# Value rows with a row sum beside each half, and the normalisation of the attention output once a chunk

## The chip, the cores and the metric

The kernel runs on one core of a Trainium2 chip. TensorE (PE) multiplies matrices into PSUM, VectorE (DVE) and ScalarE (ACT) compute on SBUF and PSUM, GpSimd (POOL) makes masks and issues some transfers, and SyncE (SP) issues most transfers. Each engine works through its own queue in order. The metric is device time in microseconds; less is better.

## What is computed

Two independent layers share the launch, and their results stand side by side in the output. The first is causal attention with a sliding window of 256 positions, 32 heads of 32 columns, 2048 positions:

```
qkv = (x @ wqkv).reshape(B, S, 3, H, Dh)
scores = einsum("bhqd,bhkd->bhqk", q, k) * Dh**-0.5
mask = (i - j >= 0) & (i - j < 256)
p = softmax(where(mask, scores, -1e9));  o = einsum("bhqk,bhkd->bhqd", p, v)
a = o.reshape(B, S, D) @ wo
```

The second is a Fourier mixing layer by matrices: a product along the hidden axis (real and imaginary part), then one along the sequence, of which the real part is kept:

```
a = x @ dft_hid_re.T;  b = x @ dft_hid_im.T
y = dft_seq_re @ a - dft_seq_im @ b
```

All is wanted to float32 precision. The kernel splits a float32 operand into two f16 parts, high and low, and forms three of the four products of parts (PASSES, L45).

## The kernel before

The work falls into stages on TensorE. First come the query, key and value projections (function `product`, L341, called from the loop at L710). Their results are split into high and low parts and written to scratch in DRAM: queries and keys to `qs`, values to `vs`. Then come the units of the Fourier layer (loop at L916): for each of two passes p (real, imaginary) and two column halves c, eight hidden-axis units `x` (`product` again, tile `p`) and eight sequence units `c` (function `seven`, L813, tiles `p_a`, `p_b`, `p_c`, a scheme of seven instead of eight block products). Last come the units of the output projection (`po_a`, `po_b`, `po_c`).

Attention is woven into these stages. It is a generator (`attention`, L175), and `tick` (L325) advances it by one step after a given number of matmuls of the other work. It goes through blocks of 128 queries for a pair of heads, in the order group of four heads (8), chunk of 512 positions (4), head pair (2), block in the chunk (4): 256 blocks, 32 chunks of eight blocks.

For a block, `s_step` (L197) forms the scores in PSUM, VectorE masks and takes the row maximum (L222, L224), ScalarE takes the exponential in place (L234) and copies the high half to f16 (L237), VectorE forms the low half (L238), and SyncE issues a transposing transfer of both halves into the tile `t` (L240). Three blocks later `z_step` (L243) lets POOL mask the edges of the window (L252, L254). Six blocks later (LAG, L39) `v_step` (L258) works on two blocks at a time: TensorE multiplies the transposed weights by the value rows `vt` (L282).

A value row of a head has 65 columns: low half (32), high half (32), and a one. High weights multiply all 65 columns; low weights multiply the last 33, high half and one. So after the products a PSUM row of 65 holds two partial results of 32 and the sum of the weights. VectorE then takes the reciprocal of the sums (L288), adds the two partial results, PSUM to PSUM (L290), and multiplies by the reciprocal into the chunk's tile `o` in SBUF (L293). The value bank has one buffer (`ps_v`, tag "pv"), shared with the small transposes `pt_...` by which scales are found (L147, L148).

After a chunk, `o_step` (L298) splits `o` into high and low f16 parts (ScalarE L302, VectorE L303), SyncE issues a transposing transfer (L305) and a store to the scratch `ots` (L306), from which the output projection reads much later.

The value rows are made at L720 to L733: POOL writes the ones (L726), ScalarE the high half (L729), VectorE the low half (L730), and SyncE stores them (L732). `do_load` brings them back a chunk at a time (L193).

The order of instructions in each engine's queue is laid out by a planner, which simulates the whole program with costs of its own (`schedule_with_timeline_sim`, L1021); `issue_after` pins a few pairs. In the sequence units of all but the first group (first pass, first column half), POOL also issues the transfers that add onto the output (L909).

Of the kernel before, what the change touches and what calls it, by code (L numbers as in the profile page):

```python
# [9 lines left out]
F32 = mybir.dt.float32  # L10
F32R = mybir.dt.float32r
F16 = mybir.dt.float16
# [3 lines left out]
AF = mybir.ActivationFunctionType  # L16
ALU = mybir.AluOpType
AX = mybir.AxisListType

P = 128  # L20
# [3 lines left out]
DH = 32  # L24
HG = 4
# [3 lines left out]
CH = 512  # L29
NCH = S // CH  # L30
QB = CH // P
VW = 2 * DH + 1
SCALE = DH ** -0.5
PSHIFT = 15.0 * math.log(2.0)
NEG = -1.0e30
# [1 line left out]
WARM = 32  # L37

LAG = 6  # L39
VW = 2 * DH + 1  # L40

# [7 lines left out]
def fused_kernel(ctx: ExitStack, tc: tile.TileContext, xa, wqk, wv, wo, xb, wd, cs, out):  # L51
    nc = tc.nc
    PSUM = bass.MemoryType.PSUM

    qs = tc.dram_tile((2, NG, NCH, 2, P, CH), F16, name="qs")
    vs = tc.dram_tile((NT, P, H * VW), F16, name="vs")
    ots = tc.dram_tile((NCH, P, NG, 2, CH), F16, name="ots")
# [35 lines left out]
    def bank(name):  # L93
        nbank[0] += 1
        return ps_m.tile([P, CH], F32, tag=f"m{nbank[0] % 3}", name=name)
# [9 lines left out]
    def vec(f, *args, **kwargs):  # L105
        with tc.issue_after(latest[0].ins) if strict[0] and latest else nullcontext():
            latest[:] = [f(*args, **kwargs)]
        return latest[0]
# [15 lines left out]
    behind = []  # L124
# [50 lines left out]
    def attention():  # L175
        att = cell["att"]
# [3 lines left out]
        st, cur, q2s, k2s, vts = {}, {}, {}, {}, {}  # L180

        def do_load(g, sc):
            if (g, sc) in q2s:
                return
            for d, kind, parts, bufs in ((k2s, 1, (0, 0, 1), 3), (q2s, 0, (0, 1, 0), 2)):
                u = att.tile([96, HG, CH], F16, tag=f"qk{kind}", bufs=bufs, name=f"qk{kind}_{g}_{sc}")
                for j, part in enumerate(parts):
# [3 lines left out]

            vt = att.tile([P, QB, HG * VW], F16, tag="vt", bufs=3, name=f"vt_{g}_{sc}")
            nc.sync.dma_start(vt, vs[sc * QB:sc * QB + QB, :, g * HG * VW:(g + 1) * HG * VW]  # L193
                              .rearrange("t p c -> p t c"))
# [63 lines left out]
        def v_step(b):  # L258

            g, sc, hp, i = blocks[b]  # L260
            pvb = ps_v.tile([P, CH], F32, tag="pv", name=f"pv_{b}")
            pvt = pvb[:, :4 * VW].rearrange("p (r h w) -> p r h w", r=2, h=2)
            if (g, sc) not in cur:
                cur[g, sc] = att.tile([P, QB, P], F32, tag="o", bufs=3, name=f"o_{g}_{sc}")
            for r in (1, 0):
                qb = sc * QB + i + r
                nb = min(qb + 1, 3)
                nt = min(nb, 2)
                d = st[b + r]

                def weights(part, j, kb):
                    if nb == 3 and kb == 0:
                        return d["z"][:, part * 2 + j]
                    return d["t"][:, (part * 2 + j) * nt + kb - (nb - nt)]

                seq = [(0, kb) for kb in range(nb)] + [(1, kb) for kb in range(nb)]
                for j in range(2):
                    at = (2 * hp + j) * VW
                    for m, (part, kb) in enumerate(seq):
                        lo = DH * part  # L280
                        k = qb + 1 - nb + kb
                        nc.tensor.matmul(pvt[:, r, j, lo:], weights(part, j, kb),  # L282
                                         vts[g, k // QB][:, k % QB, at + lo:at + VW],
                                         start=(m == 0), stop=(m == len(seq) - 1),
                                         skip_group_check=True)
            o = cur[g, sc]
            rs = att.tile([P, 2, 2], F32, tag="rs", name=f"rs_{b}")
            nc.vector.reciprocal(rs, pvt[:, :, :, 2 * DH])  # L288
            os_ = pvb[:, 4 * VW:4 * VW + 4 * DH].rearrange("p (r h d) -> p r h d", r=2, h=2)
            nc.vector.tensor_reduce(os_.rearrange("p r h d -> p (r h) d"),  # L290
                                    pvt[:, :, :, :2 * DH].rearrange("p r h (k d) -> p (r h) d k", k=2),
                                    axis=AX.X, op=ALU.add)
            nc.vector.tensor_tensor(  # L293
                o[:, i:i + 2, hp * 64:hp * 64 + 64].rearrange("p r (h d) -> p r h d", d=DH), os_,
                rs.unsqueeze(3).to_broadcast([P, 2, 2, DH]), op=ALU.mult)
            del st[b], st[b + 1]

        def o_step(g, sc):  # L298

            o = cur.pop((g, sc)).rearrange("p i c -> p (i c)")  # L300
            ohl = att.tile([P, 2, CH], F16, tag="o", bufs=3, name=f"ohl_{g}_{sc}")
            nc.scalar.activation(ohl[:, 0], o, AF.Copy)  # L302
            nc.vector.tensor_tensor(ohl[:, 1], o, ohl[:, 0], op=ALU.subtract)  # L303
            ot = att.tile([P, 2 * QB, P], F16, tag="o", bufs=3, name=f"ot_{g}_{sc}")
            nc.sync.dma_start_transpose(ot, ohl.rearrange("p h c -> p (h c)"))  # L305
            nc.sync.dma_start(ots[sc, :, g].rearrange("c h t -> c (h t)"), ot.rearrange("p a q -> p (a q)"))  # L306

        for b in range(nblk + LAG):
            for j in range(2):
# [6 lines left out]
                if j == 0 and b % 2 == 0 and b >= LAG:  # L316
                    v_step(b - LAG)
                    g, sc, hp, i = blocks[b - LAG + 1]
# [22 lines left out]
    def product(ps, lhs, rhs, n=ND, gate=None):  # L341

        m = 0
        for d in range(n):
            for hl, hr in PASSES:
                with tc.issue_after(gate.ins) if gate and 2 * d == n else nullcontext():
                    nc.tensor.matmul(ps, lhs(hl, d), rhs(hr, d), start=(m == 0), stop=(m == 3 * n - 1))  # L347
                m += 1
                if m % 8 == 0:
                    tick(8)  # L350
# [146 lines left out]
    behind_act = []  # L497
# [51 lines left out]
    for n in range(len(scans)):  # L549
        at(21 + n, scan_load, n)  # L550
        at(22 + n, scan_top, n)
        key, _, _, i, k = scans[n]
# [156 lines left out]
    with tc.tile_pool(name="pa", bufs=2) as pa:  # L709
        for n, (kd, g, c) in enumerate(order):  # L710
            if n == 4:
                first_cm.__exit__(None, None, None)
                att_cm = tc.tile_pool(name="att", bufs=2, side="right")
                cell["att"] = att_cm.__enter__()
            if n == START:
                agen[0] = attention()
                upcoming[0] = next(agen[0])
            for f, args in tasks.pop(n, ()):
                f(*args)
            ps = bank(f"p{kd}{g}_{c}")  # L720
            if kd == "v":
                t = c
                product(ps, lambda h, d: xin[:, t // 4, h, d, t % 4 * P:t % 4 * P + P],
                        lambda h, d: reg2[:, g, h, d])
                y = pa.tile([P, H // 2, VW], F16, tag="yv", name=f"yv{g}_{t}")
                nc.gpsimd.memset(y[:, :, 2 * DH:], 1.0)  # L726
                f = vf[:, g, t // 4:t // 4 + 1]
                pv = ps.rearrange("p (h d) -> p h d", d=DH)
                behind_act[:] = [nc.scalar.activation(y[:, :, DH:2 * DH], pv, AF.Copy, scale=f)]  # L729
                behind[:] = [nc.vector.scalar_tensor_tensor(y[:, :, :DH], pv, f, y[:, :, DH:2 * DH],  # L730
                                                            op0=ALU.mult, op1=ALU.subtract)]
                nc.sync.dma_start(vs[t, :, g * (H // 2) * VW:(g + 1) * (H // 2) * VW],  # L732
                                  y.rearrange("p h w -> p (h w)"))  # L733
            else:
                u = wun[kd, g]
                product(ps, lambda h, d: u[:, h, d], lambda h, d: xin[:, c, h, d], gate=gates.get(n))
                y = pa.tile([P, 2, CH], F16, tag="yq", name=f"y{kd}{g}_{c}")
                f = DOWN if kd == "q" else kf[:, c:c + 1]
                behind_act[:] = [nc.scalar.activation(y[:, 0], ps, AF.Copy, scale=f)]
                behind[:] = [vec(nc.vector.scalar_tensor_tensor, y[:, 1], ps, f, y[:, 0],  # L740
                                 op0=ALU.mult, op1=ALU.subtract)]
                nc.sync.dma_start(qs["qk".index(kd), g, c].rearrange("j p t -> p j t"), y)
            if kd == "v" and g == 0 and c % 4 == 3:
                ready.add((0, c // 4))
            if kd == "v" and g == 1 and c == NT - 1:
                pass
            if kd == "k" and g > 0:
                ready.add((g, c))
# [31 lines left out]
    os_, oq = {}, {}  # L780
# [69 lines left out]
    with tc.tile_pool(name="pb", bufs=1) as pb:  # L850
# [65 lines left out]
        for n, (kind, p, c, i) in enumerate(units):  # L916
            if kind == "x":
                x = uns.pop(n)
                tb = ytile()
                k = i % 4  # L920
# [10 lines left out]
                else:  # L931
                    a = pair.pop()
# [23 lines left out]
            f = fu.pop(n)  # L956
# [68 lines left out]
```

## Time and profile before

| | us |
|---|---|
| median of three runs | 1834.63 |
| lowest and highest | 1828.07, 1836.04 |
| span of the profiled execution | 1822.3 |
| PE busy | 1756.3 (96%) |
| DVE busy | 1325.8 (73%) |
| ACT busy | 1093.0 (60%) |
| POOL busy | 406.9 (22%) |

The profile comes from one execution. Its span runs from the first to the last instruction; the execution's own whole time is not on the page, and the median of the runs lies 12.3 us above the span. An engine that is busy is not always useful, and one that idles is not always in the way: what counts is where TensorE, the busiest engine, waits, and what ends the wait. Groups of instructions are named by line, engine and operation, with "out<-in" by the program's tile names. The mean granted clock of TensorE is 0.989 of full speed.

### The profile page before, as it was taken

To read this page: it belongs to the slowest core of one execution; us is meant where nothing else is said; L and a number is where in the kernel's file an instruction comes from. 1 tells how busy PE (TensorE), PEld (TensorE's weight loads), DVE (VectorE), ACT (ScalarE), POOL (GpSimd) and SP (SyncE) were. 2 spreads that over 40 slices of the span, in tenths; PEclk is the share of its full clock that TensorE was granted. 3 is DMA by queue.
4 is the path that set the end of the run, shared out by engine and by line. 5 is a ranking of instruction groups with operands and counts; after the bars stand their busy time and mean duration, and the time that the engine had idled before them with its cause. 6 is when DMAs were issued, how large, how long until landed. Compare 5 with 4: busy or idle time off the path is not lost.

```text
span 1822.3 us, 30052 instructions
## 1 busy us (share of the span) xinstructions
PE 1756.3 (96%) x10876; PEld 857.3 (47%) x10876; DVE 1325.8 (73%) x2362; ACT 1093.0 (60%) x1867; POOL 406.9 (22%) x666
## 2 busy tenths in 40 slices
PE   7999999999999999999989899998989999999998
PEld 3444545555545544555444444544544554444443
DVE  7665887778766788886788686888876788577442
ACT  3333554556556777776777676777776678463322
POOL 0000222222212222322123233323333223200000
PEclk9999999999999999999999999999999999999999
DMA  5357898978767656899548989756998746855331
GB/s 231 115 176 209 211 249 216 237 176 215 183 144 166 128 123 156 183 197 214 111 100 173 197 182 199 162 127 128 188 176 191 151 93 128 226 109 98 110 93 70
DMA packets 440598, 297.96 MB, mean 164 GB/s; under 512 B 339072, under 2 KB 396416, under 8 KB 440448
## 3 DMA queue, kind: packets, MB, share of 16 engines
q1 hardware_dynamic: 433536, 270.87, 62.1%
q0 software_dynamic: 6912, 25.17, 8.4%
q8 instruction: 85, 1.39, 0.3%
q14 instruction: 65, 0.53, 0.1%
HBM read 146.93 MB, written 75.63 MB: 122 GB/s over the span
## 4 chain that ended last, share of the span: by engine, by line
PE 73%; DVE 9%; issue 7%; DMA 6%; ACT 4%; POOL 2%; SPq 0%; POOLq 0%; DVEq 0%; ACTq 0%
PE p L347 13%; PE p_a L825 10%; PE pv L347 9%; PE pk L347 9%; PE pq L347 8%; PE p_b L825 5%; PE po_a L825 5%; DMA t<-hl 3%; PE s L214 3%; PE pv L282 3%; PE p_c L825 3%; PE po_b L825 2%; PE po_c L825 1%; DVE raw_u L626 1%; DMA out_dram<-reg 1%
## 5 line engine op out<-in xcount | busy, mean ns | idle before, releaser
L347 PE MATMUL p<-reg,un 128*128 128x512 f16 x1536 | 345.1, 379 | 0.0
L234 ACT ACTIVATE s<-s,bias,escs 128x256 f32<-128x256 f32 (+1 forms) x512 | 267.4, 528 | 10.6
L227 ACT ACTIVATE bias<-mx,pshift,escs 128x2 f32<-128x2 f32 x256 | 97.5, 383 | 242.7 <-DVE mx L224 210.8
L231 POOL TENSOR_SCALAR mark<-bias 128x1 f32<-128x1 f32 x128 | 42.8, 334 | 846.0 <-ACT bias L227 831.5
L347 PEld LDWEIGHTS <-un 128*128 128x128 f16 x1536 | 146.5, 98 | 164.9
L238 DVE TENSOR_TENSOR hl<-s,hl 128x512 f16<-128x512 f32 (+1 forms) x256 | 169.7, 666 | 74.5 <-ACT hl L237 72.5
L825 PE MATMUL p_a<-reg,un_c 128*128 128x512 f16 x768 | 186.0, 384 | 6.4 <-ACT p_c L832 4.9
L347 PE MATMUL pq<-reg,wu_q 128*128 128x512 f16 x768 | 177.8, 386 | 6.9 <-ACT reg L113 4.3
L254 POOL TENSOR_SCALAR_AFFINE_SELECT t<-t 128x512 f16<-128x512 f16 x224 | 181.2, 881 | 0.1
L347 PE MATMUL pk<-reg,wu_k 128*128 128x512 f16 x768 | 175.1, 379 | 0.9 <-ACT wu_k L113 0.5
L347 PE MATMUL pv<-reg,reg 128*128 128x512 f16 x768 | 174.0, 379 | 0.0
L224 DVE TENSOR_REDUCE mx<-s 128x2 f32<-128x512 f32 (+1 forms) x256 | 169.5, 666 | 2.4
L252 POOL TENSOR_SCALAR_AFFINE_SELECT z<-t 128x512 f16<-128x512 f16 x224 | 155.4, 712 | 48.9 <-DMA t<-hl 48.3
L237 ACT ACTIVATE hl<-s 128x512 f16<-128x512 f32 (+1 forms) x256 | 148.3, 583 | 9.8 <-DMA t<-hl 5.0
L222 DVE COPY_PREDICATED s<-upper,s 128x256 f32<-128x256 uint32 x224 | 94.0, 422 | 60.1 <-PE s L214 55.5
L214 PE MATMUL s<-qk,qk 96*128 96x128 f16 (+2 forms) x704 | 128.7, 276 | 3.4 <-DVE hl L238 3.4
L282 PE MATMUL pv<-vt,t 128*128 128x65 f16 x1984 | 114.3, 186 | 11.6 <-POOL t L254 11.2
L347 PEld LDWEIGHTS <-wu_q 128*128 128x128 f16 x768 | 75.3, 99 | 96.0 <-issue 13.2
L825 PEld LDWEIGHTS <-un_a 128*128 128x128 f16 x768 | 74.8, 99 | 93.1 <-issue 8.5
L825 PEld LDWEIGHTS <-un_c 128*128 128x128 f16 x768 | 74.4, 99 | 92.6 <-issue 10.2
L825 PEld LDWEIGHTS <-un_b 128*128 128x128 f16 x768 | 73.4, 98 | 89.2 <-issue 5.3
L282 PEld LDWEIGHTS <-t 128*128 128x128 f16 x1984 | 97.8, 97 | 35.1 <-POOL t L254 14.9
(175 smaller groups left out, 2873.1 us busy)
## 6 DMA issues: line engine op xcount, KB each, us to landing
raw_u<-in_cs_dram SPq DMA_DIRECT2D x64, 512.0 KB, 4.8
qk<-qs SPq DMA_DIRECT2D x192, 128.0 KB, 3.2
out_dram<-y POOLq DMA_DIRECT2D x36, 512.0 KB, 7.5
raw_u<-in_xb_dram SPq DMA_DIRECT2D x32, 512.0 KB, 5.2
vs<-yv SPq DMA_DIRECT2D x32, 260.0 KB, 2.8
vt<-vs SPq DMA_DIRECT2D x32, 260.0 KB, 4.3
raw_x<-in_xa_dram SPq DMA_DIRECT2D x16, 512.0 KB, 10.2
qs<-yq SPq DMA_DIRECT2D x32, 256.0 KB, 2.2
```

What stands on the lines that cost most here:

```text
L214: nc.tensor.matmul(s[:, j, at:at + (k1 - k0) * P], q2s[g, sc][:, h, i * P:i * P + P], k2s[g, k0 // QB][:, h, k0 % QB * P:k0 % QB * P + (k1 ...
L222: nc.vector.copy_predicated(s[:, :, 2 * P:3 * P], upper2, s[:, :, :P] if nb == 3 else never2)
L224: nc.vector.tensor_reduce(mx, sv, axis=AX.X, op=ALU.max, negate=True)
L227: nc.scalar.activation(bias, mx, AF.Identity, bias=pshift, scale=es)
L234: nc.scalar.activation(sv[:, h], sv[:, h], AF.Exp, bias=bias[:, h:h + 1], scale=es)
L237: nc.scalar.activation(hi, sv, AF.Copy)
L238: behind[:] = [nc.vector.tensor_tensor(lo, sv, hi, op=ALU.subtract)]
L252: nc.gpsimd.affine_select(out=z, in_=pk, compare_op=ALU.is_gt, fill=0.0, base=0, pattern=[[0, 4], [-1, P]], channel_multiplier=1)
L254: nc.gpsimd.affine_select(out=pk, in_=pk, compare_op=ALU.is_ge, fill=0.0, base=0, pattern=[[0, 4], [1, P]], channel_multiplier=-1)
L282: nc.tensor.matmul(pvt[:, r, j, lo:], weights(part, j, kb), vts[g, k // QB][:, k % QB, at + lo:at + VW], start=(m == 0), stop=(m == len(se ...
L347: nc.tensor.matmul(ps, lhs(hl, d), rhs(hr, d), start=(m == 0), stop=(m == 3 * n - 1))
L825: nc.tensor.matmul(ps, lhs[pos](hl, k), rhs(pos)[:, hr, k], start=(m == 0 and pos < 2), stop=(m == 11), skip_group_check=True)
```

## The change

A value row of a head becomes 66 columns: high half (32), one, low half (32), zero. High weights multiply all 66 columns; low weights the first 33. The two halves of a PSUM row then have the same form, 32 partial results and a partial sum of weights, the second of which is zero. One VectorE addition over the two halves gives results and sum of weights together, 33 columns a head, and writes them to the chunk's tile `o` in SBUF, which grows from 128 to 4 x 33 columns a block. The reciprocal and the multiplication move from `v_step`, where they ran for every two blocks, to `o_step`, where they run once a chunk, in place, over all four blocks and four heads. POOL fills the zero column with a second memset.

```diff
-VW = 2 * DH + 1
+VW = 2 * DH + 2
...
-                cur[g, sc] = att.tile([P, QB, P], F32, tag="o", bufs=3, name=f"o_{g}_{sc}")
+                cur[g, sc] = att.tile([P, QB, HG, DH + 1], F32, tag="o", bufs=3, name=f"o_{g}_{sc}")
...
-                        lo = DH * part
+                        w = VW if part == 0 else DH + 1
                         k = qb + 1 - nb + kb
-                        nc.tensor.matmul(pvt[:, r, j, lo:], weights(part, j, kb),
-                                         vts[g, k // QB][:, k % QB, at + lo:at + VW],
+                        nc.tensor.matmul(pvt[:, r, j, :w], weights(part, j, kb),
+                                         vts[g, k // QB][:, k % QB, at:at + w],
...
-            rs = att.tile([P, 2, 2], F32, tag="rs", name=f"rs_{b}")
-            nc.vector.reciprocal(rs, pvt[:, :, :, 2 * DH])
-            os_ = pvb[:, 4 * VW:4 * VW + 4 * DH].rearrange("p (r h d) -> p r h d", r=2, h=2)
-            nc.vector.tensor_reduce(os_.rearrange("p r h d -> p (r h) d"),
-                                    pvt[:, :, :, :2 * DH].rearrange("p r h (k d) -> p (r h) d k", k=2),
+            nc.vector.tensor_reduce(o[:, i:i + 2, 2 * hp:2 * hp + 2], pvt.rearrange("p r h (k w) -> p r h w k", k=2),
                                     axis=AX.X, op=ALU.add)
-            nc.vector.tensor_tensor(
-                o[:, i:i + 2, hp * 64:hp * 64 + 64].rearrange("p r (h d) -> p r h d", d=DH), os_,
-                rs.unsqueeze(3).to_broadcast([P, 2, 2, DH]), op=ALU.mult)
...
         def o_step(g, sc):
-            o = cur.pop((g, sc)).rearrange("p i c -> p (i c)")
-            ohl = att.tile([P, 2, CH], F16, tag="o", bufs=3, name=f"ohl_{g}_{sc}")
+            o = cur.pop((g, sc)).rearrange("p i h w -> p (i h) w")
+            rs = att.tile([P, HG * QB], F32, tag="rs", name=f"rs_{g}_{sc}")
+            nc.vector.reciprocal(rs, o[:, :, DH])
+            o = o[:, :, :DH]
+            nc.vector.tensor_tensor(o, o, rs.unsqueeze(2).to_broadcast([P, HG * QB, DH]), op=ALU.mult)
+            ohl = att.tile([P, 2, HG * QB, DH], F16, tag="o", bufs=3, name=f"ohl_{g}_{sc}")
             nc.scalar.activation(ohl[:, 0], o, AF.Copy)
             nc.vector.tensor_tensor(ohl[:, 1], o, ohl[:, 0], op=ALU.subtract)
...
-                nc.gpsimd.memset(y[:, :, 2 * DH:], 1.0)
+                nc.gpsimd.memset(y[:, :, DH:DH + 1], 1.0)
+                nc.gpsimd.memset(y[:, :, 2 * DH + 1:], 0.0)
...
-                behind_act[:] = [nc.scalar.activation(y[:, :, DH:2 * DH], pv, AF.Copy, scale=f)]
-                behind[:] = [nc.vector.scalar_tensor_tensor(y[:, :, :DH], pv, f, y[:, :, DH:2 * DH],
+                behind_act[:] = [nc.scalar.activation(y[:, :, :DH], pv, AF.Copy, scale=f)]
+                behind[:] = [nc.vector.scalar_tensor_tensor(y[:, :, DH + 1:2 * DH + 1], pv, f, y[:, :, :DH],
```

More of the change, by code (lines that the diff above doesn't have):

```diff
@@ L39 @@
 LAG = 6
-VW = 2 * DH + 1
+VW = 2 * DH + 2
 PASSES = ((0, 0), (0, 1), (1, 0))
@@ L304, in o_step @@
             ot = att.tile([P, 2 * QB, P], F16, tag="o", bufs=3, name=f"ot_{g}_{sc}")
-            nc.sync.dma_start_transpose(ot, ohl.rearrange("p h c -> p (h c)"))
+            nc.sync.dma_start_transpose(ot, ohl.rearrange("p a i d -> p (a i d)"))
             nc.sync.dma_start(ots[sc, :, g].rearrange("c h t -> c (h t)"), ot.rearrange("p a q -> p (a q)"))
```

## The prediction

> **What bounds the kernel now.** I read the page's first and fourth parts, then stage by stage the busy time of each engine, then who waits for whom on TensorE and on SyncE's queue, and last the groups whose instructions the change touches. First the page:
>
> ```profile
> span 1822.3 us, 30052 instructions
> PE 1756.3 (96%) x10876; PEld 857.3 (47%) x10876; DVE 1325.8 (73%) x2362; ACT 1093.0 (60%) x1867; POOL 406.9 (22%) x666
> ...
> PE 73%; DVE 9%; issue 7%; DMA 6%; ACT 4%; POOL 2%; SPq 0%; POOLq 0%; DVEq 0%; ACTq 0%
> ```
>
> TensorE is busy 96% of the span and carries 73% of the chain that ended last; the changed lines are all on VectorE, which carries 9%. So the change can only pay through the 66 us in which TensorE stands still (1822.3 - 1756.3). Where those lie (columns: stretch, length, then busy time of PE, PEld, DVE, ACT, POOL with instruction counts, granted clock, DMA share and rate):
>
> ```profile
> 682.00:832.00 150.00, 149.28 (x1003) 75.33 (x1003) 124.45 (x241) 117.71 (x209) 42.18 (x64) 1.00 0.82 188
> 909.00:1136.00 227.00, 206.89 (x1374) 101.84 (x1373) 179.25 (x326) 160.66 (x281) 74.61 (x101) 0.98 0.84 168
> 1136.00:1215.00 79.00, 79.00 (x539) 39.64 (x536) 66.70 (x115) 57.68 (x100) 24.57 (x37) 1.00 0.69 148
> 1215.00:1402.00 187.00, 173.86 (x1143) 86.02 (x1141) 145.25 (x285) 137.30 (x250) 60.00 (x89) 0.96 0.84 167
> 1402.00:1511.00 109.00, 109.00 (x727) 54.62 (x724) 82.74 (x142) 76.85 (x135) 30.38 (x47) 1.00 0.61 130
> 1511.00:1662.00 151.00, 140.58 (x767) 65.56 (x764) 114.45 (x184) 95.03 (x138) 28.84 (x38) 0.99 0.67 148
> 180.00:1662.00 1482.00, 1436.15 (x9429) 714.10 (x9427) 1145.58 (x2119) 992.46 (x1733) 402.10 (x642) 0.99 0.77 169
> ```
>
> From 180 us, where attention starts, to 1662 us TensorE idles 45.9 us (1482.00 - 1436.15). Three stages of sequence-transform units hold 43.7 of them: 20.1 in 909-1136, 13.1 in 1215-1402, 10.4 in 1511-1662. The first such stage, 682-832, idles 0.7 us although VectorE is busier there (124.45 of 150, 83%) than in 909-1136 (79%). VectorE's load alone therefore does not make the stalls. What ends them (total us, times, longest):
>
> ```profile
> PE pv L282 <- POOL t L254: 11.2, 11, 2.2
> PE pv L282 <- POOL z L252: 11.1, 4, 6.1
> PE p_a L825 <- DVE y L819: 5.8, 7, 1.8
> PE p_a L825 <- ACT p_c L832: 4.9, 7, 1.4
> PE s L214 <- DVE hl L238: 3.4, 5, 1.0
> PE pt_u L148 <- DVE o L293: 2.2, 1, 2.2
> ...
> POOL z L252 <- DMA t<-hl: 48.3, 28, 6.6
> ```
>
> The largest are value products waiting for POOL's masks (22.3 us in 15 waits), and POOL in turn waits 48.3 us for transposed tiles, which SyncE's queue issues. VectorE is named for some 11 us. One of these, 2.2 us, is the changed code itself: a scale transpose needs the value bank that the old normalisation still holds.
>
> **The change, part by part.** These are the groups (busy us, mean ns of one | idle before):
>
> ```profile
> L288 DVE RECIPROCAL rs<-pv 128x4 f32<-128x4 f32 x128 | 22.3, 174 | 25.0 <-PE pv L282 24.8
> L290 DVE TENSOR_REDUCE pv<-pv 128x128 f32<-128x256 f32 x128 | 54.3, 424 | 1.2
> L293 DVE TENSOR_TENSOR o<-pv,rs 128x128 f32<-128x128 f32 x128 | 36.3, 284 | 1.6
> L224 DVE TENSOR_REDUCE mx<-s 128x2 f32<-128x512 f32 x240 | 163.0, 682 | 2.2
> L224 DVE TENSOR_REDUCE mx<-s 128x2 f32<-128x256 f32 x16 | 6.7, 416 | 0.2
> L107 DVE RECIPROCAL sc_u<-sc_u 128x1 f32<-128x1 f32 x32 | 5.1, 160 | 0.7
> L626 DVE TENSOR_TENSOR r<-r,r 128x512 f32<-128x512 f32 x24 | 16.6, 690 | 0.7
> L626 DVE TENSOR_TENSOR raw_u<-raw_u,raw_u 128x512 f32<-128x512 f32 x96 | 72.3, 753 | 0.5
> L302 ACT ACTIVATE ohl<-o 128x512 f16<-128x512 f32 x32 | 20.1, 628 | 11.1 <-DVE o L293 11.1
> L303 DVE TENSOR_TENSOR ohl<-o,ohl 128x512 f16<-128x512 f32 x32 | 25.1, 785 | 10.4 <-ACT ohl L302 10.0
> L282 PE MATMUL pv<-vt,t 128*128 128x65 f16 x992 | 101.8, 194 | 11.6 <-POOL t L254 11.2 <-DVE sc_u L107 0.4
> L282 PE MATMUL pv<-vt,z 128*128 128x65 f16 x448 | 80.4, 192 | 11.1 <-POOL z L252 11.1
> L214 PE MATMUL s<-qk,qk 96*128 96x384 f16 x256 | 66.6, 328 | 0.0
> L214 PE MATMUL s<-qk,qk 96*128 96x128 f16 x224 | 43.4, 219 | 2.1 <-DVE hl L238 2.1
> L726 POOL MEMSET yv<- 128x16 f16 x32 | 5.5, 170 | 262.8 <-DMA vs<-yv 238.8 <-DVE pv L290 8.0 <-DVE s L222 7.5
> ```
>
> Removed from VectorE: 128 reciprocals (22.3 us) and 128 multiplies (36.3 us), 58.6 us. Added, once in each of 32 chunks: a reciprocal of 16 elements, between 160 ns (one element from SBUF) and some 20 ns over the 174 ns of four; I take 0.18 us, 5.8 us in all. And a 512-element multiply with both inputs in SBUF: between 690 and 753 ns by the two nearest rows; I take 0.72, 23.0 us. The sum grows from 256 to 264 inputs: the two L224 rows give (682 - 416) / 256 = 1.04 ns an element, so 8 ns, 128 times, 1.0 us; that it now writes SBUF costs nothing by the row of 416 ns, which writes SBUF from 256 inputs, beside 424. VectorE's sum: -58.6 + 5.8 + 23.0 + 1.0 = -28.8 us, ends -30.4 and -27.1. That is 2.5% of its 1145.6 us.
>
> TensorE: 992 + 448 = 1440 products take 66 columns instead of 65; the other half keep 33. The two score rows give (328 - 219) / 256 = 0.43 ns a column, so +0.6 us, on the path. The low end is 0, where a column hides behind the fixed part of a product.
>
> The bank of the value products is freed after one VectorE instruction, not three. The next value products come a block pair later, so they gain nothing; the 2.2 us of the scale transpose go. What is late next there is the sum itself, already done.
>
> The rest of the gain comes from VectorE's queue. In the three stalled stages it is busy 438.95 of 565 us, 77.7%; 2.5% less is 75.8%. I let the stall scale as busy over idle share (3.48 to 3.13, -10%): of 43.7 - 2.2 us that is -4.3. This scaling is my choice; its ends are 0 (stage 682-832 shows a fuller VectorE without stalls) and half of the 43.7 us, 21.9.
>
> The chunk's end gets longer: ScalarE's copy (L302) now waits for reciprocal and multiply, 0.90 us more, and behind it stand VectorE's subtraction (L303), the transposing issue L305 and the store L306 on SyncE. During the burst VectorE holds back masks and maxima of the blocks in flight. ScalarE already waits 11.1 us here. SyncE's queue (total us, times, longest):
>
> ```profile
> SPq L240 <- DVE hl L238: 259.5, 115, 7.8
> ...
> SPq L305 <- DVE hl L238: 21.0, 7, 7.0
> ...
> SPq L305 <- DVE mx L224: 13.4, 6, 5.2
> ...
> SPq L305 <- DVE y L819: 12.0, 1, 12.0
> ```
>
> While SyncE stands at L305, the transposes of later blocks (L240) stand behind it. The old multiply runs from the first to the last pair of blocks (durations min/median/max, first and last start):
>
> ```profile
> L293 DVE TENSOR_TENSOR o<-pv,rs x128: 271/281/292, 185.9 to 1564.2; 128x128 f32<-128x128 f32 x128
> ```
>
> A chunk so takes (1564.2 - 185.9) / 32 = 43 us, and of the stalled stages 909-1136, 1215-1402 and 1511-1564 hold attention: about 11 chunk ends. I charge each with 0.90 us times the share of time in which TensorE idles there (43.7 / 565 = 7.7%): +0.8 us. Ends: 0, where six blocks of lag cover it, and the rival below. Copy and subtraction read rows of 32 at a stride of 33; I take 628 and 785 ns unchanged.
>
> At nothing: 32 more memsets of 170 ns (5.4 us), hidden by a POOL that is busy 22% and there already waits 238.8 us for earlier stores; uncovered they would delay a store, not a product. Value rows grow by 1.5% in store and load, some 0.07 us on a transfer a chunk ahead of its use. The smaller bank and the larger chunk tile hold the same buffer counts.
>
> Sum: -2.2 - 4.3 + 0.6 + 0.8 = -5.1 us, a span of 1817. The page gives this execution's span alone; the median of the runs, 1834.6, is 12.3 us above it, and I carry that distance over: **1829.5 us**.
>
> One stall costs more than its idle time:
>
> ```profile
> 1238.00:1243.00 5.00, 2.37 (x43) 1.70 (x42) 3.31 (x11) 3.23 (x7) 0.21 (x1) 1.00 0.85 184
> 1243.00:1250.00 7.00, 5.73 (x19) 1.84 (x16) 6.90 (x14) 4.89 (x9) 2.73 (x4) 0.52 0.34 64
> ```
>
> After the stall that holds the scale transpose, the granted clock is 0.52 for 7 us. I leave this out of the sum, because other stalls may take that place. [...]
>
> **The rivals.** *The stalls largely go (faster).* They cascade: a late mask, an idle TensorE, a half clock. If relief breaks half of them, 21.9 us less and +1.4: 1814. For it: the 0.7 us of stage 682-832 shows that such a stage can run dry of stalls. Against it: 22.3 us of the waits name POOL, whose work is unchanged.
>
> *The chunk's end stalls SyncE (slower).* The longer chain holds L305, the next blocks' transposes come late, POOL's masks too, and value products wait. Price: 11 chunk ends at the 1.5 us of a present wait on POOL (22.3 / 15), 16.5 us, with the queue's gain lost: +16.5 - 2.2 + 0.6, 1849.5. It makes the kernel slower by over 0.5% from (9.2 + 5.9) / 11 = 1.4 us an end. For it: SyncE waited 12.0 us once at L305; against it: the lag of six blocks.
>
> *VectorE's relief is hidden anyway.* All stalls come from POOL, SyncE and ScalarE: 1835.
>
> *The new multiply holds POOL.* A mask's duration (min/median/max):
>
> ```profile
> L254 POOL TENSOR_SCALAR_AFFINE_SELECT t<-t x224: 626/638/2299, 183.7 to 1554.2; 128x512 f16<-128x512 f16 x112
> ```
>
> Something stretches single masks from 638 to 2299 ns. The multiply is there 32 times for 0.72 us; POOL is busy 402.10 of 1482 us, 27%, so 8 or 9 would meet a mask; if 8 times 0.72 us reach TensorE whole, that is 5.8 us, and the time is 1835. [...]
>
> **How the numbers follow.** Each queue's order is laid out by a planner from simulated times, so every stage is reshuffled; that two like stages idle 0.7 and 20.1 us bounds what this can do, and is why the rivals are wide. Chances: forecast 0.40 (0.10 of it beyond 9.2 us faster), stalls go 0.22, SyncE 0.22, hidden 0.11, POOL 0.05. The runs of before spread over 8 us, so 0.5%, 9.2 us, is about what can be told. Faster 0.10 + 0.22 = 0.32; slower 0.22; same 0.46. The range takes in most of both outer cases, 1812 to 1850; the forecast's own is 1822 to 1834.
>
> **What would show it.** Right: the sum at 0.43 us, 128 times; 32 multiplies near 0.72; VectorE's busy time near 1297; no scale transpose waiting for L293's successor; idle TensorE in the three stages near 38 us. Wrong: SyncE's waits at L305 growing beyond 4 us each (SyncE rival), masks beside the multiply over 1 us (POOL rival), stalls in stages that have none now, or idle time in the three stages under 25 us.

## The result, and the profile after

The changed kernel takes 1843.19 us (median of 6 runs, 1838.08 to 1847.52) against 1833.41 us for the kernel before (6 runs): a ratio of 1.0068, 95% interval 1.0044 to 1.0093. It is slower, by a little more than the 0.5% that the prediction set as the bound of what can be told; 1829.5 us were forecast. The time lies inside the stated range, on the other side of no change.

The head of the page of the changed kernel. Its profiled execution is the slowest of its six, 1847.52 us:

```profile
span 1845.8 us, 29830 instructions
PE 1765.1 (96%) x10876; PEld 858.1 (46%) x10876; DVE 1309.1 (71%) x2170; ACT 1091.4 (59%) x1867; POOL 415.2 (22%) x698
```

VectorE did get less to do (1309.1 us, from 1325.8), and yet the span grew. TensorE stands still for 80.7 us of it (1845.8 - 1765.1), where it stood still for 66.0 before. The same stages as in the prediction, at the times at which they now run, so with somewhat other bounds (PE, PEld, DVE, ACT, POOL busy, granted clock, DMA):

```profile
668.00:834.00 166.00, 163.40 (x1089) 81.56 (x1088) 133.88 (x242) 130.87 (x232) 44.17 (x70) 1.00 0.73 178
930.00:1127.00 197.00, 175.37 (x1090) 84.18 (x1088) 145.02 (x250) 134.76 (x237) 59.88 (x81) 0.95 0.84 165
1135.00:1231.00 96.00, 91.84 (x631) 45.59 (x630) 69.59 (x110) 65.19 (x114) 35.27 (x47) 1.00 0.73 142
1231.00:1421.00 190.00, 173.35 (x1133) 85.12 (x1132) 146.09 (x263) 136.99 (x249) 59.39 (x88) 0.96 0.86 165
1421.00:1517.00 96.00, 96.00 (x627) 47.87 (x626) 70.82 (x110) 64.98 (x113) 27.80 (x42) 1.00 0.62 131
1517.00:1690.00 173.00, 157.58 (x876) 73.78 (x875) 129.10 (x199) 105.65 (x159) 34.39 (x44) 0.99 0.69 139
180.00:1690.00 1510.00, 1449.30 (x9447) 716.92 (x9445) 1132.93 (x1931) 991.14 (x1734) 410.56 (x665) 0.99 0.77 166
```

While attention runs, TensorE now idles 60.7 us (1510.00 - 1449.30); it was 45.9. The three sequence-unit stages hold 53.7 of them (21.6, 16.7, 15.4), and the stage of hidden-axis units at 1135-1231, where the first profile showed a TensorE that never idled (1136-1215), has 4.2. What ends TensorE's waits, over the whole span (total us, times, longest):

```profile
PE pv L282 <- POOL z L252: 17.3, 11, 4.7
PE pv L282 <- POOL t L254: 10.8, 11, 2.0
PE s L214 <- DVE hl L238: 6.0, 5, 1.9
...
PE p_a L823 <- ACT p_c L830: 5.2, 4, 2.2
...
PE pt_u L148 <- DVE o L287: 1.5, 2, 1.2
```

The waits for POOL's masks are more numerous (22, were 15) and sum to 28.1 us (were 22.3). The groups that the change made or touched:

```profile
L287 DVE TENSOR_REDUCE o<-pv 128x132 f32<-128x264 f32 x128 | 54.6, 427 | 32.4 <-PE pv L282 32.1
L297 DVE TENSOR_TENSOR o<-o,rs 128x512 f32<-128x512 f32 x32 | 24.6, 770 | 0.5
L295 DVE RECIPROCAL rs<-o 128x16 f32<-128x16 f32 x32 | 7.9, 247 | 0.3
L282 PE MATMUL pv<-vt,z 128*128 128x66 f16 x448 | 80.6, 192 | 17.4 <-POOL z L252 17.3
L724 POOL MEMSET yv<- 128x16 f16 x32 | 6.1, 194 | 0.0
```

The sum costs what it was priced at; the reciprocal (247 ns, 180 taken) and the multiply (770, 720 taken) cost VectorE some 4 us more in all. That is too little to explain the loss by itself: where TensorE waits, the instructions are mostly those of before. What changed around them is their order. The planner laid out the queues anew. The order of TensorE's 10876 matmuls first differs at the 823rd; 5456 of them stand elsewhere, and the average over all is 6.6 places. VectorE's instructions stand 1.9 places off, ScalarE's 1.6, SyncE's 0.6; POOL's hardly differ.

### The profile page after: what moved, and what is told of

Its sections match the earlier page's. It is cut to its first block, busy times and chain, and to the rows that moved or that the text cites. A ratio compares the mean times of both kernels' runs of the same rounds, so it can differ in the third digit from the quotient of the medians.

```text
span 1845.8 us, 29830 instructions
## 1 busy us (share of the span) xinstructions
PE 1765.1 (96%) x10876; PEld 858.1 (46%) x10876; DVE 1309.1 (71%) x2170; ACT 1091.4 (59%) x1867; POOL 415.2 (22%) x698
## 4 chain that ended last, share of the span: by engine, by line
PE 65%; issue 12%; DVE 11%; DMA 5%; ACT 4%; POOL 3%; POOLq 0%; SPq 0%; DVEq 0%; ACTq 0%
PE p L344 11%; PE pv L344 9%; PE pk L344 9%; PE pq L344 8%; PE p_a L823 8%; PE po_a L823 5%; PE p_b L823 4%; DMA t<-hl 3%; PE s L214 3%; PE pv L282 3%; PE p_c L823 2%; PE po_b L823 2%; POOL t L254 1%; POOL z L252 1%; DVE raw_u L623 1%
## 5 line engine op out<-in xcount | busy, mean ns | idle before, releaser
L231 POOL TENSOR_SCALAR mark<-bias 128x1 f32<-128x1 f32 x128 | 51.7, 404 | 884.9 <-ACT bias L227 861.5
L254 POOL TENSOR_SCALAR_AFFINE_SELECT t<-t 128x512 f16<-128x512 f16 x224 | 179.3, 885 | 0.1
L222 DVE COPY_PREDICATED s<-upper,s 128x256 f32<-128x256 uint32 x224 | 94.2, 424 | 74.2 <-PE s L214 68.3
L282 PE MATMUL pv<-vt,t 128*128 128x66 f16 x1984 | 117.0, 186 | 11.2 <-POOL t L254 10.8
```

The source lines that it names most:

```text
L222: nc.vector.copy_predicated(s[:, :, 2 * P:3 * P], upper2, s[:, :, :P] if nb == 3 else never2)
L254: nc.gpsimd.affine_select(out=pk, in_=pk, compare_op=ALU.is_ge, fill=0.0, base=0, pattern=[[0, 4], [1, P]], channel_multiplier=-1)
L282: nc.tensor.matmul(pvt[:, r, j, :w], weights(part, j, kb), vts[g, k // QB][:, k % QB, at:at + w], start=(m == 0), stop=(m == len(seq) - 1) ...
```

## The experiments

Two theories. **ORDER**: the changed work is harmless or a small gain, and the new layout of the queues costs the time. **WORK**: the new instructions cost it, by the longer chunk end, by the multiply with two SBUF inputs, or by the wider rows. To tell them apart, the order of a kernel must be held while its instructions change. The function below does that: after everything is traced, it links the instructions of each engine into a chain, in an order recorded from another kernel, with edges that fix the order of issue alone and add no wait for completion. With its own order, the kernel before came out with the same queues as without it, so the edges by themselves change nothing there; that program was not run on the chip. Where two kernels differ in instructions, the new sum takes the place of the old one, and the chunk's reciprocal and multiply that of the chunk's last old multiply; in the mirror (old instructions in an order recorded from new ones), reciprocal, sum and multiply stand together at the place of the sum.

```diff
+def pin(tc):
...
+    made = {}
+    for i in tc.nc.cur_bb.bb.instructions:
+        if type(i).__name__ != "BassTilePoolBoundary":
+            made.setdefault(str(i.engine).split(".")[-1], []).append(i)
+    info = mybir.DependencyInfo(mybir.DependencyClass.NoSync, mybir.DependencyReason.DATA)
+    for engine, text in ORDERS.items():
...
+        for a, b in zip(places, places[1:]):
+            tc.add_manual_dep(mine[b], mine[a].name, info, reason="pin")
...
         fused_kernel(tc, *args)
+        pin(tc)
```

### The new instructions in the old order

The edit: the changed kernel, and `pin` with the order of the kernel before for all five engines.

> The changed kernel's instructions, with every engine's queue held in the order that the kernel before had (the sum stands where the old sum stood, the chunk's reciprocal and multiply where the chunk's last old multiply stood). Theory ORDER (the change costs time only because the planner laid all queues out anew): at or below the kernel before, 1826 to 1835 us, about the -5 us of the predicted sum. Theory WORK (the new instructions themselves cost it: the longer chunk end, or the multiply with two SBUF inputs): 1840 us or more, as the changed kernel.

Measured: 1828.95 us against 1828.28 us, ratio 1.0005, interval 0.9982 to 1.0029. The loss is gone with the order alone; in the old order nothing in the new instructions costs 0.7%. Nor is the predicted gain there: -5.1 us would be 0.9972, just outside the interval. The head of its page, and TensorE's waits:

```profile
span 1818.4 us, 29823 instructions
PE 1753.6 (96%) x10876; PEld 856.1 (47%) x10876; DVE 1318.7 (73%) x2170; ACT 1093.6 (60%) x1867; POOL 418.0 (23%) x698
...
PE pv L282 <- POOL t L254: 11.8, 11, 2.4
PE pv L282 <- POOL z L252: 8.8, 4, 4.3
...
PE pt_u L148 <- DVE o L287: 1.5, 1, 1.5
...
ACT ohl L299 <- DVE o L297: 21.6, 18, 2.8
```

Value products wait for masks in 15 places, as before the change (4 and 11), where the same instructions in their own order have 22. ScalarE waits 21.6 us for the chunk's multiply, 10.5 us more than for the old one: the chunk's end is longer, as predicted, and costs nothing that can be measured.

### The old instructions in the new order

The edit: the kernel before, and `pin` with the order of the changed kernel.

> The mirror: the old instructions, with every queue held in the order of the changed kernel (reciprocal, sum and multiply together where the new sum stands). Theory ORDER: 1843 us or more, some 5 us above the changed kernel, since it keeps the bad order and has more VectorE work. Theory WORK: near the kernel before, 1830 to 1836 us.

Measured: 1862.42 us, ratio 1.0194, interval 1.0165 to 1.0224. The old instructions lose 34 us by the new order, far more than the changed kernel, whose order it is. In this order the new instructions are thus the better ones: 1.0194 beside 1.0068, although the two ratios come from different chips.

```profile
span 1860.5 us, 30036 instructions
PE 1768.2 (95%) x10876; PEld 858.2 (46%) x10876; DVE 1343.0 (72%) x2362; ACT 1089.8 (59%) x1867; POOL 408.0 (22%) x666
...
PE s L214 <- DVE hl L238: 9.6, 9, 1.9
...
PE pt_u L148 <- DVE o L293: 2.8, 2, 1.8
```

TensorE's waits for VectorE's low halves are 9.6 us here, against 3.4 with the same instructions in their own order. Not all of the 34 us need be the order's. VectorE is busy 1343.0 us, where the same instructions took 1325.8 in their own order, although their durations sum to nearly the same (1455.4 and 1454.5 us). Each multiply waits for its sum, and each sum for its reciprocal. In the mirror the three stand back to back all 128 times, and no sum overlaps the multiply behind it; in the old order the three stand so only 22 times, and others between them overlap with them. What this placing costs was not tried apart.

### One part alone: one normalisation a chunk

```diff
-            rs = att.tile([P, 2, 2], F32, tag="rs", name=f"rs_{b}")
-            nc.vector.reciprocal(rs, pvt[:, :, :, 2 * DH])
...
+            nc.vector.reciprocal(rcp[g, sc][:, i:i + 2, 2 * hp:2 * hp + 2], pvt[:, :, :, 2 * DH])
+            nc.vector.tensor_reduce(
+                o[:, i:i + 2, hp * 64:hp * 64 + 64].rearrange("p r (h d) -> p r h d", d=DH),
...
+            nc.vector.tensor_tensor(ov, ov, rs.unsqueeze(2).to_broadcast([P, HG * QB, DH]), op=ALU.mult)
```

> One part alone: rows of 65 columns and the reciprocal per block pair as before, but the sum goes to SBUF and one multiply a chunk normalises; the planner orders it freely. Theory WORK with the chunk end at fault: slower than before, 1840 us or more. Theory WORK with the wide rows at fault: 1828 to 1833. Theory ORDER says only that it lies somewhere within 10 us of before, on either side, by the layout of its queues.

Measured: 1820.34 us, ratio 0.9963, interval 0.9941 to 0.9984, faster than before. The multiply at the chunk's end is thus no cause of a loss in itself. Whether the gain is its work or its order is told by two runs below.

### The other part alone: wide rows

```diff
-VW = 2 * DH + 1
+VW = 2 * DH + 2
...
+                        hi = VW - part
-                        nc.tensor.matmul(pvt[:, r, j, lo:], weights(part, j, kb),
-                                         vts[g, k // QB][:, k % QB, at + lo:at + VW],
+                        nc.tensor.matmul(pvt[:, r, j, lo:hi], weights(part, j, kb),
+                                         vts[g, k // QB][:, k % QB, at + lo:at + hi],
...
-                nc.gpsimd.memset(y[:, :, 2 * DH:], 1.0)
+                nc.gpsimd.memset(y[:, :, 2 * DH:2 * DH + 1], 1.0)
+                nc.gpsimd.memset(y[:, :, 2 * DH + 1:], 0.0)
```

> The other part alone: rows of 66 columns (low, high, one, zero), 66 columns in the products with high weights, the second memset; reciprocal, sum and multiply per block pair as before. The planner keeps nearly all of the first half of its queues and changes some of the second. Theory WORK with the rows at fault: 1840 us or more. By the predicted terms alone: +0.6 us, 1834. Theory ORDER: within 10 us of before on either side, although the work is nearly the same.

Measured: 1844.12 us, ratio 1.0086, interval 1.0054 to 1.0117. By itself this reads as WORK, with the rows at fault: one column in half of the products, and nearly 1% lost. The next run shows that the reading would be wrong.

### The kernel before in the order of the wide rows

The edit: the kernel before, rows of 65 columns, and `pin` with the order of the kernel with wide rows.

> The kernel before, unchanged in its instructions (rows of 65 columns), with every queue held in the order that the planner gave the kernel with wide rows alone (1.0086 of before). Theory ORDER: as slow as that kernel, 1840 us or more (ratio 1.006 to 1.011). Theory WORK (the wide rows cost it): 1828 us, ratio 1.00.

Measured: 1841.02 us, ratio 1.0066, interval 1.0040 to 1.0092. Not one instruction differs from the kernel before, and none had to be given a place by hand; only the order differs, and it costs 0.7%. Of the 1.0086 that leaves the rows 0.2%, which lies within the intervals.

```profile
span 1842.8 us, 30062 instructions
PE 1760.4 (96%) x10876; PEld 859.0 (47%) x10876; DVE 1328.2 (72%) x2362; ACT 1093.6 (59%) x1867; POOL 408.6 (22%) x666
...
PE pv L282 <- POOL z L252: 18.6, 9, 6.1
PE pv L282 <- POOL t L254: 13.4, 9, 2.4
PE s L214 <- DVE hl L238: 10.5, 8, 4.2
```

The engines' busy times are those of the kernel before (VectorE 1328.2 beside 1325.8, POOL 408.6 beside 406.9), while the waits for masks are 32.0 us instead of 22.3 and those for low halves 10.5 instead of 3.4.

### Both, in the order of one normalisation a chunk

The edit: the changed kernel, and the kernel before, each with `pin` and the order of the kernel with one normalisation a chunk.

> The changed kernel's instructions, with every queue held in the order that the planner gave the kernel with one normalisation a chunk (0.9963 of before). Theory ORDER: 1815 to 1824 us, ratio 0.993 to 0.998, 20 us below the same instructions in their own order. Theory WORK: 1840 us.

> The kernel before in that same order. If the order alone gives the gain of one normalisation a chunk: 1818 to 1824 us. If that order needs the smaller VectorE load it was laid out for, as the mirror run suggests (old instructions in the new order were 19 us slower than the new ones): 1835 us or more.

Measured: the changed instructions take 1820.63 us, ratio 0.9951 (0.9933 to 0.9969); the old ones 1835.32 us, ratio 1.0031 (1.0016 to 1.0046). The change as it was asked for, in another order, thus beats the kernel before by 0.5%, and beside the 1.0068 of its first form, measured on another chip, it is better by more than 1%. In this one order, on one chip, the changed instructions are 0.8% faster than the old ones (0.9951 beside 1.0031). The old ones stand back to back here too, nearly always (121 of 128), so this 0.8% holds the price of that placing (VectorE busy 1346.2 us). The heads of the two pages, and the waits of the changed instructions:

```profile
span 1815.0 us, 29820 instructions
PE 1751.1 (96%) x10876; PEld 854.1 (47%) x10876; DVE 1314.2 (72%) x2170; ACT 1093.7 (60%) x1867; POOL 409.0 (23%) x698
...
PE pv L282 <- POOL z L252: 14.1, 11, 3.2
PE pv L282 <- POOL t L254: 7.8, 9, 1.9
```

```profile
span 1829.3 us, 30019 instructions
PE 1757.3 (96%) x10876; PEld 855.6 (47%) x10876; DVE 1346.2 (74%) x2362; ACT 1092.6 (60%) x1867; POOL 402.3 (22%) x666
```

No wait of a score product for a low half stands in the changed instructions' list any more (6.0 us in the changed kernel's own order). TensorE stands still for 63.9 us, hardly less than the 66.0 of the kernel before. Most of the gain is clock: full speed less the mean granted clock, times the span, is 15.0 us on average over the 12 runs, and 23.2 over the 29 runs of the kernel before on that chip, 8.2 of the 10.0 us by which the mean times differ.

### One normalisation a chunk in the old order

The edit: the kernel of the third experiment, and `pin` with the order of the kernel before.

> The kernel with one normalisation a chunk, in the order of the kernel before. If its gain of 0.4% is the order's: ratio 1.00, 1828 us. If it is the work's (VectorE's load, shorter hold of the value bank): 1820 us, ratio 0.996.

Measured: 1836.76 us, ratio 1.0034, interval 1.0013 to 1.0054. Neither expectation holds: it is not faster by its work, and in the old order it is slower than the old instructions are. The kernel before and this one do best in their own orders (1.0000 and 0.9963); the changed kernel does not (1.0068 in its own, 0.9951 at best). So, in these runs, the planner's order fits a kernel only by chance or in part.

| instructions | order before | order changed | order wide | order norm a chunk |
|---|---|---|---|---|
| before | 1.0000 | 1.0194 | 1.0066 | 1.0031 |
| changed | 1.0005 | 1.0068 | | 0.9951 |
| wide rows | | | 1.0086 | |
| norm a chunk | 1.0034 | | | 0.9963 |

Each ratio is to the kernel before on the same chip.

### Which queue

The edit: the changed kernel, with `pin` for one engine alone and the order of the kernel before; the planner lays out the other four.

> The changed kernel with SyncE's queue alone held in the order of the kernel before; the planner lays out the others, and they come out as far from the old order as in the changed kernel (mean place on TensorE 6.9 instructions off, on VectorE 1.9). If SyncE's order (transposes behind other transfers) makes the loss: ratio 1.000 to 1.002. If it is the others': 1.005 to 1.009.

> The changed kernel with VectorE's queue alone held in the old order; the others then come out nearer to it (TensorE 2.4 instructions off, ScalarE 0.4, SyncE 0.1). If VectorE's order makes the loss: ratio near 1.000. If TensorE's remaining differences do: 1.004 or more.

> The changed kernel with TensorE's queue alone held in the old order; VectorE's comes out 0.3 instructions off, ScalarE's 0.2, SyncE's 0.1. If the places of the scores and value products in TensorE's queue make the loss: ratio 1.000, as with all queues held. If small differences on the other queues suffice to move the time: anything between 0.995 and 1.010.

Measured: SyncE's queue alone 1.0054 (1.0034 to 1.0074), VectorE's alone 1.0158 (1.0115 to 1.0201), TensorE's alone 1.0041 (1.0016 to 1.0066). SyncE's order does not carry the loss: with the old one most of it stays. VectorE's old order, with the other queues planned around it, is worse than either whole layout. With TensorE's queue held, the other queues differ from the old ones by a third of a place or less on average, and still some 0.4% are left. So none of these three queues gives the whole loss back alone. That it hangs on how the queues fit each other is likely, but argued: the planner lays out the other four around the held one, so no run has one old queue among four new ones, and ScalarE's and POOL's were not held alone. Which single displaced instructions begin the waits stays open. A shorter lead from scores to value products is not the rule. The lead is taken as the TensorE work that stands between the last score product of a pair of blocks and its first value product (matmuls at the median pitch of their kind in the trace). Of the leads after 575 us, the tenth percentile is 16.3 us before and 13.3 in the changed kernel, but 16.4 in the slow wide rows and 14.1 in the fast kernel with one normalisation a chunk.

## Why the prediction was wrong

**The sign.** The step that failed is the one that treats the planner: the text says that every stage is reshuffled, takes this as width for the rivals, and makes the sum as if the order stayed. With the order held, the change costs nothing (1.0005, where the sum gives 0.9972); the 0.7% come from the order. The two idle times that the prediction itself quoted, 0.7 and 20.1 us for like stages, were the warning: a new order alone can make a loss or a gain, and it had no case of its own.

**How the loss adds up.** The same instructions in the two orders, by the profiled executions (spans 1845.8 and 1818.4 us, a difference of 27.4; one is the slowest of its runs and the other the fastest, the ratios of the runs give 0.6%, some 11 us). TensorE stands still for 80.7 and 64.8 us, +15.9. By what ends the waits: POOL's masks 28.1 and 20.6, +7.5; ScalarE 19.8 and 12.0, +7.8; VectorE 27.8 and 27.1. The other 11.5 us are in TensorE's busy time, 1765.1 and 1753.6, and most of that is clock. Its mean granted value, in that order:

```profile
core 0: 1845.8 us, clock 0.986
```

```profile
core 0: 1818.4 us, clock 0.991
```

0.014 of 1845.8 and 0.009 of 1818.4 us are 25.8 and 16.4 us of lost clock, +9.5. But this part comes of setting a slow execution beside a fast one, and is not the order's. In both kernels the clock lies between 0.986 and 0.991 from run to run, and the lost clock is 21.8 us on average over the six runs of the changed kernel and 20.3 over the twelve of the other, +1.5. So the loss is in the main standing still, and the clock's share, which the prediction had left out of its sum, did not make it. Within one execution the clock is lower in stages with more idle time: 0.95 and 0.96 in the two where TensorE idles 21.6 and 16.7 us, 0.99 where it idles 15.4, 1.00 where it idles 4.2 or less. In the prediction's rows it is 1.00 over the 5 us in which TensorE idles 2.6 (5.00 - 2.37), and 0.52 over the next 7. What sets such a drop off, and what ends it, these runs do not show.

**VectorE's relief was too large: -28.8 us forecast.** In the old order it is 1318.7 - 1325.8 = -7.1. Two rates were low: the reciprocal of 16 elements takes 247 ns (0.18 us taken, at most some 0.19 allowed), the multiply 770 on average (720 taken, 753 the upper end; why is told under the masks below). By the rows of the changed kernel that gives -58.6 + 7.9 + 24.6 + 0.3 = -25.8. The rest is in the main a fault of the method. Instructions on VectorE overlap, as the timeline of the kernel before shows (start, length):

```profile
1239.51 0.18 DVE L288 RECIPROCAL rs<-pv 128x4 f32<-128x4 f32 x1
1239.61 0.68 DVE L224 TENSOR_REDUCE mx<-s 128x2 f32<-128x512 f32 x1
```

The next one starts 0.08 us before the end of the one in front. In the kernel before, 1600 of its 2362 VectorE instructions are so overlapped by the next, by 0.08 us in the median: their durations sum to 1454.5 us, 128.7 more than the busy time. With the new instructions in the old order, the durations sum to 1433.6 us, 20.9 less (other groups took some 5 us longer), and the overlaps to 114.8, 13.9 less. The difference of the two is the -7. Time that an instruction spends beside another is counted as saved by a sum of durations, and was never spent.

**The scaling of stalls by VectorE's load** (-4.3 us) is not confirmed. In the old order, less VectorE work changes nothing measurable. In the order of one normalisation a chunk, the new instructions gain 0.8% on the old ones, more than the scaling gave, but there the old ones stand back to back.

**The 2.2 us of the scale transpose** shrank to 1.5 and did not go. "The sum itself, already done" was wrong: the transpose now waits for the sum (L287).

**TensorE's +0.6 us and the memsets at nothing** are too small to be told: the products of 66 columns take 192 ns, as those of 65 did, and with the old order the whole change is within 0.3% of zero.

**The chunk's end.** Of the +0.8 us on the path nothing can be seen. As a rival, a stall of SyncE, it fell. SyncE's waits at the transposing issue (now L302) sum to 68.8 us, against 88.5 before; the largest rows:

```profile
SPq L302 <- DVE y L623: 12.9, 2, 10.9
SPq L302 <- DVE s L222: 10.3, 5, 6.0
SPq L302 <- DVE hl L238: 8.6, 4, 3.6
```

They should have grown beyond 4 us each. They fell, and the kernel was slower all the same: the right sign for the wrong reason. With the new instructions in the old order these waits sum to 94.2 us, a little more than before, and the time does not grow. It was the price of this rival that took the range up to 1850, so it is luck that the range holds the 1843.

**The multiply that holds POOL** did hold it, and it cost nothing. The masks that the prediction showed (L254) keep their median:

```profile
L254 POOL TENSOR_SCALAR_AFFINE_SELECT t<-t x224: 627/637/3168, 183.9 to 1584.1; 128x512 f16<-128x512 f16 x112
```

But the median says nothing of the few masks that meet a multiply. One such pair in the changed kernel (start, length):

```profile
466.12 0.69 DVE L297 TENSOR_TENSOR o<-o,rs 128x512 f32<-128x512 f32 x1
466.18 1.12 POOL L252 TENSOR_SCALAR_AFFINE_SELECT z<-t 128x512 f16<-128x512 f16 x1
```

Of the 448 masks, 16 meet a new multiply, and 12 of these take over 1 us, the sign that the prediction named; of the 69 that met an old multiply, which read PSUM, 13 did. The multiply suffers as well: the 22 that meet no mask take 677 to 694 ns, the ten that meet one 681 to 1122. So the 690 ns of the prediction's lower row is right for a multiply alone, and the mean of 770 comes of the meetings, ten of 32 (the prediction reckoned 8 or 9). All in all no more masks are long than before (93 over 1 us, 100 before), since other VectorE work meets them too: of the 47 that met one of the L626 instructions on `raw_u` with two inputs in the kernel before, 29 took over 1 us. And the price is not there: in the old order 14 of 23 masks that meet a multiply take over 1 us, and the time is that of the kernel before (1.0005). So much is measured: both are longer where they meet. What the two engines then wait for, these runs do not show.

## What to carry to other kernels

Where a planner orders the queues, a change of a few instructions is a change of the whole order, and the order can be worth more than the change: here the same instructions ran from 0.9951 to 1.0068 of the old time in three whole layouts, and the untouched old ones from 1.0000 to 1.0194 in four (to 1.0066 where none stood at a place given by hand). Judge such a change with the order held, and if the work pays, look for a better order before giving the change up. And a small part tried alone proves nothing while the order moves with it: the wide rows seemed to cost 0.9%, and the kernel without them, in their order, cost 0.7%.

## What the runs showed of the hardware

In the kernel before, 1600 of 2362 VectorE instructions are overlapped by the next, by 0.08 us in the median; in the mirror, none of the 128 sums is overlapped by the multiply right behind it, which waits for it. So the busy time that the new instructions saved in the old order (7.1 us) was less than the fall in the durations (20.9), and the old instructions kept VectorE busy for 1325.8 us in their own order, where others mostly stand between reciprocal, sum and multiply, and for 1343.0 in the mirror, where none do. A VectorE multiply of 512 elements with both inputs in SBUF took some 692 ns where it met no GpSimd mask (median of 22) and up to 1122 where it met one (ten), and masks of 637 ns in the median took over 1 us beside it in 12 of 16 cases. A reciprocal of 16 elements in SBUF at a stride of 33 took 247 ns, where one of 4 elements in PSUM took 174. The 12 runs of one kernel on one chip spread over 1% (1820.08 to 1838.29 us for the first experiment). The granted clock of these two runs is 0.991 and 0.986, which makes some 9 of the 18 us. So two profiled executions should not be compared by their clock without the clocks of the other runs.
